# The first quad's second head pair: loaded as fp32 by two other queues and cast on VectorE

## The chip, the cores and the metric

The kernel runs on one core of one Trainium2 chip. The metric is the device time of one execution in microseconds (us). Five engines run their own instruction streams: TensorE (PE in the profile; PEld is its weight load), VectorE (DVE), ScalarE (ACT), GpSimd (POOL) and SyncE (SP). DMAs are issued from the queues of POOL, SP and ScalarE. Only those issued by POOL convert a type on the way here; the ones that SP and ScalarE issue at the start move fp32 as it is.

## The reference

Attention with an extra one in the softmax's sum, over 8 batches, 12 heads, 448 positions, head size 64, followed by a feed-forward layer with squared ReLU:

```python
scores = scale * np.matmul(q, k.transpose(0, 1, 3, 2))
m = np.max(scores, axis=-1, keepdims=True)
e = np.exp(scores - m)
attn = e / (np.sum(e, axis=-1, keepdims=True) + np.exp(-m) + 1e-09)
x = (attn @ v).transpose(0, 2, 1, 3).reshape(B * S, H * D)   # 3584 x 768
h = x @ w_in                                                 # 768 x 2048
g = np.maximum(h, 0.0) ** 2
out = g @ w_out                                              # 3584 x 768, fp32
```

The inputs are fp32; the kernel multiplies in fp16.

## The kernel before, in words

The 12 heads of a batch are three quads of four heads; a quad has two head pairs, j = 0 and 1, and in a pair the two heads lie in partitions 0 to 63 and 64 to 127. For scores, q and k are needed with the head size in the partitions, so TensorE transposes them by matmuls against an identity (`ident`), and VectorE or ScalarE copies the result from PSUM to the tile `qk`.

The order of all work is written out by hand. Each step in the text `ORDER` (line 858) is a letter and its numbers, and each engine takes its own instructions of these steps in that order; a wait stands in the engine's way of everything behind it. The steps of the start that matter here (name 0 is q, 1 is k):

- `load_first_quad` (L121): SP loads q and ScalarE loads k of the first quad's pair j = 0, in two pieces each (columns 0 to 255, 256 to 447), as fp32, into the tile `raw`, which is an exponential tile (`et`) used early.
- `load_first_second` (L128): POOL loads q and k of pair j = 1 of the first quad, cast to fp16 on the way, to `flatq` and `flatk`. Then POOL makes the identity.
- `d0`, `d8`, `d1` and so on: further POOL loads. `d0` loads q and k of quad 1 of batch 0 (tile `nn`), `d8` v of quad 0, `d1` quad 2.
- `c` (`first_cast`, L220): casts a piece of `raw` to fp16, on ScalarE (last number 1) or VectorE (0).
- `t n,j,c` (`first_transpose`, L229): TensorE transposes a piece of pair j, with one idle matmul ahead; `u n,j,c,act` (`first_copy`, L238): the copy out of PSUM. The transposes use two PSUM buffers in turn.
- `s n` and `e n`: the scores of one piece (`half_scores`) and their exponential on ScalarE (`half_exp`, L255). Steps 0 to 3 and 12 to 15 are the first quad's (s0 and s1 need only pair 0, s2 and s3 pair 1; 12 on belong to the second half of the queries). The scores have two PSUM buffers.
- `T0,1,n` and `U`: transposes of quad 1's q and k out of `nn` (L208) and their copies (L218). They come behind s12 and ahead of s3 in TensorE's order.
- `b`, `y`, `z`, `n`, `x`, `p`: the sums, reciprocals and products with v of each half quad.

Behind this start the matmuls of attention, of `w_in` and of `w_out` of several batches are woven together; later batches are loaded through fp16 copies in DRAM and transposed by DMA.

Of the kernel before, what the change touches and what calls it, by code (L numbers as in the profile page):

```python
# [10 lines left out]
FP32 = mybir.dt.float32  # L11
FP16 = mybir.dt.float16
# [5 lines left out]
def kernel(  # L18
# [9 lines left out]
    nc = tc.nc  # L28

    B, H, S, D = q.shape  # L30
# [4 lines left out]
    RUN = 4  # L35
    NQ = H // 4
    KC = S // 64
# [16 lines left out]
    flat = ctx.enter_context(tc.tile_pool(name="flat", bufs=2))  # L54
    qk_pool = ctx.enter_context(tc.tile_pool(name="qk", bufs=2))
    e_pool = ctx.enter_context(tc.tile_pool(name="e", bufs=4))
# [18 lines left out]
    by_pairs = {n: t.rearrange("b (hp i) (p t) d -> b (i p) hp (t d)", i=2, t=KC)  # L75
                for n, t in (("q", q), ("k", k), ("v", v))}
# [4 lines left out]
    vns, qks, xts, naturals, stages = {}, {}, {}, {}, {}  # L81
# [37 lines left out]
                naturals[name, b, g] = parts[:, x, n].rearrange("p j (c d) -> p j c d", d=D)  # L119

    def load_first_quad():  # L121
        raw = e_pool.tile([128, RUN * S], FP32, name="et")[:, 0:2 * S].rearrange("p (n x) -> p n x", n=2)
        for c0, c1 in ((0, 4 * D), (4 * D, S)):
            nc.sync.dma_start(out=raw[:, 0, c0:c1], in_=by_pairs["q"][0, :, 0, c0:c1])
            nc.scalar.dma_start(out=raw[:, 1, c0:c1], in_=by_pairs["k"][0, :, 0, c0:c1])
        return raw.rearrange("p n (c d) -> p n c d", d=D)

    def load_first_second():  # L128
        for name in "qk":
            f = naturals[name, 0, 0, 1] = flat.tile([128, KC, D], FP16, name=f"flat{name}")  # L130
            nc.gpsimd.dma_start(out=f.rearrange("p c d -> p (c d)"), in_=by_pairs[name][0, :, NQ])

    def load_win(i, n):
        w = DF // n
# [82 lines left out]
        else:  # L217
            nc.vector.tensor_copy(dst, src)  # L218

    def first_cast(raw, name, c0, c1, act):  # L220
        if (name, 0, 0, 0) not in naturals:
            naturals[name, 0, 0, 0] = flat.tile([128, KC, D], FP16, name=f"flat{name}")
        f, src = naturals[name, 0, 0, 0][:, c0:c1], raw[:, "qk".index(name), c0:c1]
        if act:
            nc.scalar.activation(out=f, in_=src, func=AF.Copy)
        else:
            nc.vector.tensor_copy(f, src)

    def first_transpose(which, j, c0, c1):  # L229
        rows_ = slice(64 * j, 64 * j + 64)  # L230
        tp = tps[which, j, c0] = mp_tile(FP16)
        x, n = 64 - 64 * j, 128 * (c1 - c0)
        mm(aside()[x:x + 64, 0, 0:n], idle[:, x:x + 64], idle[:, 0:n], start=True, stop=True)
        for c in range(c0, c1):
            nc.tensor.transpose(tp[rows_, 128 * (c - c0):128 * (c - c0) + 128],
                                naturals[which, 0, 0, j][:, c, :], ident)
# [355 lines left out]
    one_b = consts.tile([128, 1], FP32)  # L592
    nc.vector.memset(one_b, 1.0 / GS)
    raw = load_first_quad()
    nc.scalar.preload_act_table_set("natural_log_exp_and_others")
    ident = consts.tile([128, 128], FP16)
    nc.vector.memset(ident, 0.0)
    load_first_second()
    make_identity(nc, ident, nomemset=True)
    NW = 4  # L600

# [4 lines left out]
    def fill(n):  # L606
        wp = mp_tile()
        for _ in range(n):
            mm(wp[:, 0:S], idle[:, 0:128], idle[:, 0:S], start=True, stop=True)
# [203 lines left out]
    def halves(b):  # L813
# [3 lines left out]
    STEPS = {  # L817
        "W": lambda n: keep_warm(n),
        "f": lambda n: fill(n),
        "c": lambda n, c, act: first_cast(raw, "qk"[n], c, KC if c else 4, act),  # L820
        "t": lambda n, j, c: first_transpose("qk"[n], j, c, KC if c else 4),
        "u": lambda n, j, c, act: first_copy("qk"[n], j, c, KC if c else 4, act),
        "T": lambda b, g, n: transpose_one(b, g, "qk"[n]),
# [30 lines left out]
    def other_ring():  # L854
# [1 line left out]
        ring.append(ctx.enter_context(tc.tile_pool(name="ring", bufs=4, space=bass.MemoryType.PSUM)))  # L856

    ORDER = """
        d0 W8 d8 d1 c1,4,0 c0,0,1 t0,0,0 c1,0,1 t1,0,0 u0,0,0,0 t1,0,4 u1,0,0,0 c0,4,1 u1,0,4,1 t0,0,4 d2 s0 t0,1,0 u0,0,4,1 u0,1,0,0 t1,1,0
        u1,1,0,0 d10 d9 s1 t0,1,4 e0 t1,1,4 e1 s2 e2 u0,1,4,0 s12 e12 u1,1,4,0 T0,1,0 T0,1,1 U0,1,0,0,4,0 U0,1,1,0,4,0 U0,1,1,4,7,0  # L860
        U0,1,0,4,7,0 s3 s4 p2 p0 e3 b0,0 e4 s6 p1 d18 p3 s5 e6 e5 b0,1 b0,2 T0,2,0 b0,3 y0 T0,2,1 U0,2,0,0,4,0 z0 n0 U0,2,1,0,4,0 b1,0 s8
        U0,2,0,4,7,0 U0,2,1,4,7,0 x0 d3 d17 d16 b1,1 s9 d15 T1,0,1 e8 e9 U1,0,1,0,7,0 T1,0,0 U1,0,0,0,7,0 b2,0 s11 e11 s10 s13 e10 e13 s14 p8
# [232 lines left out]
```

## Time and profile before

| | us |
|---|---|
| median of 3 runs | 372.48 |
| lowest, highest | 372.31, 372.57 |
| profiled execution | 372.36 |
| its span (first to last instruction) | 370.3 |
| TensorE busy in the span | 361.7 |
| ScalarE, VectorE, POOL busy | 282.4, 275.7, 62.3 |

The granted clock of TensorE was 1.00 throughout. A row of the timeline reads: start, length, engine, line, operation, tiles, shape, count, and in brackets the idle time of that engine just ahead of it with what ended it. Rows of the chain read: start, length, what. The rows of stretches give each engine's busy time, then the clock, the share of the 16 DMA engines (over 1 where packets overlap) and GB/s. The rows of DMA issues end with the size of one and the median time from issue to landing.

### The profile page before, as it was taken

How to read it: one execution, taken by the hardware profiler on the slowest of the kernel's cores; microseconds unless marked ns; L12 is line 12 of the kernel's file. 1: busy time of each engine (PE TensorE's matmuls, PEld its weight loads, DVE VectorE, ACT ScalarE, POOL GpSimd, SP SyncE). 2: the span in 40 equal slices, each digit the busy share in tenths (PEclk: the TensorE clock that was granted, in tenths of full speed). 3: DMA queues.
4: the chain of work that ended last, by engine and by line, in shares of the span. 5: the costliest groups of instructions: out<-in, count | busy, mean ns of one | idle time of the engine just before them, and what ended most of it. 6: DMA issues, size and time to landing. Idle time of an engine off the chain costs nothing.

```text
span 370.3 us, 13666 instructions
## 1 busy us (share of the span) xinstructions
PE 361.7 (98%) x6024; PEld 248.8 (67%) x6024; DVE 275.7 (74%) x484; ACT 282.4 (76%) x413; POOL 62.3 (17%) x96
## 2 busy tenths in 40 slices
PE   8789999999999999999999999999999999999996
PEld 4566556669977755567799965557777765555664
DVE  3888898999987875867887874777878777885441
ACT  6899988987899645689999665679999748794221
POOL 8543350400400330400201060400200000000000
PEclk9999999999999999999999999999999999999999
DMA  8999999999777999905229669854212110001232
GB/s 138 203 205 205 204 198 206 226 225 189 154 146 133 190 181 191 134 2 114 62 58 156 154 118 180 162 64 99 61 53 66 47 62 5 2 0 44 86 85 88
DMA packets 75052, 45.31 MB, mean 122 GB/s; under 512 B 47473, under 2 KB 72945, under 8 KB 74993
## 3 DMA queue, kind: packets, MB, share of 16 engines
q0 software_dynamic: 24752, 22.62, 38.7%
q1 hardware_dynamic: 49952, 21.59, 27.0%
q8 instruction: 47, 0.77, 0.9%
q10 hardware_dynamic: 288, 0.23, 0.2%
q14 instruction: 13, 0.10, 0.1%
HBM read 45.69 MB, written 17.93 MB: 172 GB/s over the span
## 4 chain that ended last, share of the span: by engine, by line
PE 90%; ACT 4%; DVE 2%; DMA 2%; issue 1%; POOL 1%; POOLq 0%; DVEq 0%
PE mp L94 42%; PE mp L663 38%; PE sp L94 9%; ACT et L255 3%; DMA nn<-in_k_dram 2%; PE mp L208 1%; ACT rcp L373 1%; DVE qk L218 0%; ACT rcp L366 0%; DVE half L342 0%; DVE half L441 0%; DVE half L443 0%; DVE half L445 0%; DVE half L348 0%; DVE xt L485 0%
## 5 line engine op out<-in xcount | busy, mean ns | idle before, releaser
L255 ACT ACTIVATE et<-sp 128x896 f16<-128x896 f32 (+2 forms) x173 | 145.2, 899 | 7.6 <-PE sp L94 6.9
L94 PE MATMUL mp<-wout,gs 64*64 64x384 f16 (+1 forms) x2736 | 138.8, 322 | 0.2 <-issue 0.2
L94 PEld LDWEIGHTS <-gs 64*64 64x64 f16 (+1 forms) x2736 | 87.4, 107 | 21.7 <-issue 0.8
L663 PEld LDWEIGHTS <-win 128*128 128x128 f16 x480 | 46.4, 98 | 33.6 <-issue 1.2
L94 PE MATMUL sp<-qk 64*64 64x224 f16 (+1 forms) x1056 | 56.2, 273 | 2.3 <-issue 0.7
L663 PE MATMUL mp<-xt,win 128*128 128x448 f16 (+1 forms) x288 | 54.2, 329 | 0.0
L94 PEld LDWEIGHTS <-qk 64*64 64x64 f16 x1056 | 34.4, 114 | 14.5 <-issue 6.2
L189 POOL COPY flatq<-qk 64x384 f16<-64x384 f16 x20 | 15.3, 763 | 159.4 <-DMA qk<-stage_k 142.7
L94 PE MATMUL mp<-et,vn 64*64 64x448 f16 (+1 forms) x616 | 38.8, 345 | 0.0
L663 PE MATMUL mp<-et,win 128*128 128x448 f16 x144 | 32.8, 352 | 0.0
L576 DVE TENSOR_SCALAR ot<-mp 128x384 f32<-128x384 f32 x34 | 18.9, 556 | 18.0 <-PE mp L94 17.9
L663 PE MATMUL mp<-et,nn 128*128 128x448 f16 (+1 forms) x160 | 32.3, 350 | 0.0
L663 PEld LDWEIGHTS <-nn 128*128 128x128 f16 x216 | 21.0, 98 | 14.7
L666 ACT ACTIVATE qk<-mp 128x448 f32<-128x448 f32 (+1 forms) x33 | 16.8, 532 | 16.0 <-PE mp L663 15.9
L580 DVE SCALAR_TENSOR_TENSOR ot<-mp,ot 128x384 f32<-128x384 f32 x42 | 23.4, 556 | 6.7 <-ACT ot L574 4.0
L485 DVE TENSOR_TENSOR xt<-mp,rcp 128x448 f16<-128x448 f32 x42 | 24.2, 618 | 4.3 <-ACT rcp L464 2.2
L94 PEld LDWEIGHTS <-vn 64*64 64x64 f16 x756 | 22.7, 107 | 6.1 <-issue 0.5
L715 ACT ACTIVATE gs<-mp 128x448 f16<-128x448 f32 x28 | 14.2, 543 | 15.0 <-PE mp L663 13.3
L439 DVE TENSOR_TENSOR half<-et 128x1792 f16<-128x1792 f16 x21 | 23.0, 1097 | 1.2 <-ACT et L255 1.2
L660 DVE CUSTOM_DVE_ANT_0 gs<-mp,rcp 128x448 f16<-128x448 f32 x24 | 14.2, 619 | 13.0 <-ACT rcp L666 7.4
L441 DVE TENSOR_TENSOR half<-half,et 128x1792 f16<-128x1792 f16 x21 | 22.8, 1085 | 0.7 <-DVE half L439 0.5
L710 ACT ACTIVATE gs<-gs 128x448 f16<-128x448 f16 (+1 forms) x36 | 22.4, 657 | 1.1 <-DVE gs L660 1.1
(102 smaller groups left out, 450.2 us busy)
## 6 DMA issues: line engine op xcount, KB each, us to landing
out_dram<-ot SPq DMA_DIRECT2D x52, 96.0 KB, 3.5
out_dram<-ot SPq DMA_DIRECT2D x19, 192.0 KB, 2.0
win<-in_moe_w_in_dram POOLq DMA_DIRECT2D x8, 384.0 KB, 12.9
wout<-in_moe_w_out_dram POOLq DMA_DIRECT2D x4, 768.0 KB, 11.8
vn<-in_v_dram POOLq DMA_DIRECT2D x10, 288.0 KB, 5.6
stage_q<-in_q_dram POOLq DMA_DIRECT2D x4, 676.0 KB, 11.6
stage_k<-in_k_dram POOLq DMA_DIRECT2D x4, 676.0 KB, 14.4
nn<-in_q_dram POOLq DMA_DIRECT2D x8, 224.0 KB, 7.9
```

Of the source, the lines that this page charges most:

```text
L94: return nc.tensor.matmul(out_, lhsT, rhs, start=start, stop=stop)
L189: nc.gpsimd.tensor_copy(km[rows_].rearrange("p h (x o) -> p h x o", o=2)[:, :, :, odd], src[:, :, S // 2 - 32:S // 2])
L255: nc.scalar.activation(out=out_, in_=in_, func=AF.Exp, scale=scale)
L439: nc.vector.tensor_add(esq[m], a[:, 0:w], a[:, w:2 * w])
L441: nc.vector.tensor_add(esq[m], esq[m], z[:, 0:w])
L485: nc.vector.tensor_mul(xts[b][:, 2 * g + i, :], xqs[m][i][:, 0:S], zqs[m][:, i, :])
L576: nc.vector.tensor_scalar(out=ot, in0=op[:, 0:w], scalar1=OUT_SCALE, scalar2=None, op0=ALU.mult)
L580: nc.vector.scalar_tensor_tensor(out=ot, in0=lo[:, 0:w], scalar=OUT_SCALE, in1=ot, op0=ALU.mult, op1=ALU.add)
L660: nc.vector._custom_dve(TENSOR_ADD_SAT, out=out_, in0=ps, in1=t, s0=3.0e38, s1=0.0)
L663: nc.tensor.matmul(out_, lhsT=lhsT, rhs=rhs, start=begins and first, stop=last, skip_group_check=not begins)
L666: nc.scalar.activation(out=t[:, 0:w], in_=src[:, 0:w], func=AF.Copy, scale=scale_)
L710: nc.scalar.activation(out=out_, in_=out_, func=AF.Square)
```

## The change

q and k of pair j = 1 of the first quad are no longer loaded by POOL. `raw` becomes twice as large, and SP and ScalarE each issue a third load, of 128 x 448 fp32, behind their first two. A new step `q n,act` casts one of the two to fp16 into `flatq` or `flatk`; both casts are on VectorE. q0,0 stands behind c0,4,1 and q1,0 behind d2, so on VectorE both come after the copies u0,0,0,0 and u1,0,0,0 and ahead of u0,1,0,0. POOL's first work is now the identity, and its first DMA is d0's. TensorE's order is unchanged; its first transposes of pair 1 wait for VectorE in place of a DMA.

```diff
     def load_first_quad():
-        raw = e_pool.tile([128, RUN * S], FP32, name="et")[:, 0:2 * S].rearrange("p (n x) -> p n x", n=2)
+        raw = e_pool.tile([128, RUN * S], FP32, name="et").rearrange("p (j n x) -> p j n x", j=2, n=2)
         for c0, c1 in ((0, 4 * D), (4 * D, S)):
-            nc.sync.dma_start(out=raw[:, 0, c0:c1], in_=by_pairs["q"][0, :, 0, c0:c1])
-            nc.scalar.dma_start(out=raw[:, 1, c0:c1], in_=by_pairs["k"][0, :, 0, c0:c1])
-        return raw.rearrange("p n (c d) -> p n c d", d=D)
-
-    def load_first_second():
-        for name in "qk":
-            f = naturals[name, 0, 0, 1] = flat.tile([128, KC, D], FP16, name=f"flat{name}")
-            nc.gpsimd.dma_start(out=f.rearrange("p c d -> p (c d)"), in_=by_pairs[name][0, :, NQ])
+            nc.sync.dma_start(out=raw[:, 0, 0, c0:c1], in_=by_pairs["q"][0, :, 0, c0:c1])
+            nc.scalar.dma_start(out=raw[:, 0, 1, c0:c1], in_=by_pairs["k"][0, :, 0, c0:c1])
+        nc.sync.dma_start(out=raw[:, 1, 0], in_=by_pairs["q"][0, :, NQ])
+        nc.scalar.dma_start(out=raw[:, 1, 1], in_=by_pairs["k"][0, :, NQ])
+        return raw.rearrange("p j n (c d) -> p j n c d", d=D)
...
-    def first_cast(raw, name, c0, c1, act):
-        if (name, 0, 0, 0) not in naturals:
-            naturals[name, 0, 0, 0] = flat.tile([128, KC, D], FP16, name=f"flat{name}")
-        f, src = naturals[name, 0, 0, 0][:, c0:c1], raw[:, "qk".index(name), c0:c1]
+    def first_cast(raw, name, j, c0, c1, act):
+        if (name, 0, 0, j) not in naturals:
+            naturals[name, 0, 0, j] = flat.tile([128, KC, D], FP16, name=f"flat{name}")
+        f, src = naturals[name, 0, 0, j][:, c0:c1], raw[:, j, "qk".index(name), c0:c1]
...
     nc.vector.memset(ident, 0.0)
-    load_first_second()
     make_identity(nc, ident, nomemset=True)
...
-        "c": lambda n, c, act: first_cast(raw, "qk"[n], c, KC if c else 4, act),
+        "c": lambda n, c, act: first_cast(raw, "qk"[n], 0, c, KC if c else 4, act),
+        "q": lambda n, act: first_cast(raw, "qk"[n], 1, 0, KC, act),
...
-        d0 W8 d8 d1 c1,4,0 c0,0,1 t0,0,0 c1,0,1 t1,0,0 u0,0,0,0 t1,0,4 u1,0,0,0 c0,4,1 u1,0,4,1 t0,0,4 d2 s0 t0,1,0 u0,0,4,1 u0,1,0,0 t1,1,0
+        d0 W8 d8 d1 c1,4,0 c0,0,1 t0,0,0 c1,0,1 t1,0,0 u0,0,0,0 t1,0,4 u1,0,0,0 c0,4,1 q0,0 u1,0,4,1 t0,0,4 d2 q1,0 s0 t0,1,0 u0,0,4,1 u0,1,0,0 t1,1,0
```

## The prediction

> **What bounds the kernel now.** I read the page's busy times and the summary of the chain that ended last, then that chain in order of time, then the timeline of each engine over the first 16 us, where the change sits. From the page:
>
> ```profile
> span 370.3 us, 13666 instructions
> PE 361.7 (98%) x6024; PEld 248.8 (67%) x6024; DVE 275.7 (74%) x484; ACT 282.4 (76%) x413; POOL 62.3 (17%) x96
> PE 90%; ACT 4%; DVE 2%; DMA 2%; issue 1%; POOL 1%; POOLq 0%; DVEq 0%
> ```
>
> TensorE is busy 98% of the span and holds 90% of the chain. A change at the start can therefore do one thing only: move the time at which TensorE's unbroken work begins. The chain in order of time (start, length, what):
>
> ```profile
> 1.25 0.47 POOL flatq L131
> 1.93 0.56 POOL flatk L131
> ...
> 3.59 6.19 DMA nn<-in_k_dram
> 9.83 0.60 PE mp L208 x14
> 10.45 0.95 DVE qk L218 x3
> ...
> 15.41 5.19 ACT et L255 x7
> ...
> 33.37 2.39 PE mp L94 x12
> ```
>
> The reader is to see four legs. POOL issues q and k of the first quad's second head pair (flatq, flatk), then q and k of quad 1 (nn). The load of nn's k takes 6.19 us from its issue, and TensorE's transposes of it start at 9.83. VectorE copies them out, ScalarE's exponentials carry the chain from 15.41, and TensorE has it from 33.37 to the end. So the two POOL issues that the change removes stand on the chain, ahead of the load that ends its second leg. Whether their going is worth anything depends on what the chain's next-latest neighbours are at 9.83. ScalarE:
>
> ```profile
> 1.65 1.28 ACT L595 ACT_TABLE_LOAD   x1 [1.65 <-PEq L1079]
> 3.68 0.42 ACT L225 ACTIVATE flatq<-et 128x256 f16<-128x256 f32 x1 [0.75 <-DMA et<-in_q_dram]
> 6.27 1.77 ACT L255 ACTIVATE et<-sp 128x896 f16<-128x896 f32 x3
> 8.33 1.73 ACT L255 ACTIVATE et<-sp 128x896 f16<-128x896 f32 x2 [0.29 <-PE sp L94]
> 10.86 3.22 ACT L255 ACTIVATE et<-sp 128x448 f16<-128x448 f32 x5 [0.81 <-PE sp L94]
> 15.41 5.18 ACT L255 ACTIVATE et<-sp 128x896 f16<-128x896 f32 x7 [0.18 <-PE sp L94]
> ```
>
> ScalarE works almost without a break from 6.27 on. The two exponentials of 8.33 end at 10.06; then it idles 0.81 us until 10.86 for the scores of step s3. After 10.86 there is only 0.18 us of idle time at 15.41. So the most this stage can give is 0.81 + 0.18 = 0.99 us, less what the steps before 8.33 lose. TensorE in the same stretch:
>
> ```profile
> 6.16 0.41 PE L235 MATMUL mp<-ident,flatq 128*64 128x128 f16 x4
> 6.41 0.39 PE L235 MATMUL mp<-ident,flatk 128*64 128x128 f16 x4
> 6.74 0.47 PE L94 MATMUL sp<-qk 64*64 64x224 f16 x6
> 7.14 0.35 PE L235 MATMUL mp<-ident,flatq 128*64 128x128 f16 x3
> 7.72 0.76 PE L94 MATMUL sp<-qk 64*64 64x224 f16 x16
> 8.69 0.58 PE L208 MATMUL mp<-ident,nn 128*64 128x128 f16 x14 [0.21 <-DMA nn<-in_q_dram]
> 9.83 0.58 PE L208 MATMUL mp<-ident,nn 128*64 128x128 f16 x14 [0.55 <-DMA nn<-in_k_dram]
> 10.35 0.97 PE L94 MATMUL sp<-qk 64*64 64x224 f16 x14
> ```
>
> In order: step t0,1,0 (transposes of flatq's second half pair, 6.16), t1,1,0 (flatk's, 6.41), s1 (6.73), t0,1,4 (7.14), s2 and s12 (7.72), T0,1,0 (nn's q, 8.69, which waited for its load), T0,1,1 (nn's k, 9.83, likewise), s3 (10.35). s3 reads nothing of nn: it only stands behind T0,1,1 in TensorE's order. That is why a load sets ScalarE's 0.81 us.
>
> **The change part by part.** *POOL.* Removed: two DMA issues, 0.70 + 0.56 us.
>
> ```profile
> 1.25 0.70 POOL L131 DMA_DIRECT2D flatq<-in_q_dram  x1 [0.80 <-POOLq L1079]
> 1.93 0.56 POOL L131 DMA_DIRECT2D flatk<-in_k_dram  x1
> 2.61 0.29 POOL masks.py:199 TENSOR_SCALAR_AFFINE_SELECT ident<-ident 128x128 f16<-128x128 f16 x1
> 2.86 0.74 POOL L118 DMA_DIRECT2D nn<-in_q_dram  x1
> 3.59 0.73 POOL L118 DMA_DIRECT2D nn<-in_k_dram  x1
> ```
>
> All POOL work behind them moves up by 1.26 us: the identity (2.61, needed by TensorE's first transposes, which come after the cast of 3.68) to 1.35, nn's q from 2.86 to 1.60, nn's k from 3.59 to 2.33, and the issues after them alike. POOL's later waits are for landings eight of its own DMAs back, and these move with the issues.
>
> *The loads.* The DMA engines' share by stretch (the last two columns):
>
> ```profile
> 2.00:3.00 1.00, 1.00 (x4) 0.44 (x3) 0.00 (x0) 0.93 (x1) 0.88 (x3) 1.00 0.87 259
> 3.00:4.00 1.00, 1.00 (x5) 0.26 (x3) 0.08 (x1) 0.32 (x1) 1.00 (x2) 1.00 1.20 281
> 4.00:5.00 1.00, 0.87 (x11) 0.57 (x12) 0.81 (x3) 0.66 (x3) 1.00 (x2) 1.00 1.10 107
> ```
>
> The plain fp32 loads ran at 259 to 281 GB/s mixed with others; the engines were already at a share of 1.10 to 1.20 from 3 us. The removed and the added loads read the same 2 x 229 KB, so the engines' work until nn's k is complete stays about as it was, and only the 1.26 us of issue is gained, at most: nn's k at 9.78 - 1.26 = 8.5 us; at least nothing (9.8), if the engines are the limit throughout. I take about 9.0, between the two, as the share of 1.10 is nearer to full. nn's q was late at 8.69 and comes by 7.4 to 8.7.
>
> The new loads are the third issue on SP's and ScalarE's queues. A pair of issues takes 0.90 us there, so the third goes out at about 0.74 + 0.90 = 1.6 and ends near 2.1. On ScalarE it pushes the table load from 1.65 to 2.1, ending at 3.4: hidden behind the wait until 3.68 (0.75 us of idle time, of which 0.45 is used; without that cover it would cost 0.45).
>
> ```profile
> 0.74 0.90 SPq L124 DMA_DIRECT2D et<-in_q_dram  x2
> et<-in_q_dram SPq DMA_DIRECT2D x1, 128.0 KB, 2.9
> flatk<-in_k_dram POOLq DMA_DIRECT2D x1, 112.0 KB, 4.0
> ```
>
> The first two loads of each queue are done by 4.0 (the cast at 3.92). The new ones follow in the same queues: 459 KB at 281 GB/s is 1.6 us, so from about 3.7 to 5.3 with nn's q sharing the engines. Bounds: 1.6 + 2.9 = 4.5 by the fp32 rows' time to landing; 1.6 + 5.8 = 7.4 if they take as long as nn's q did (2.86 to 8.69). I take 5.4; the removed flatk, on the more crowded queue, would give 1.6 + 4.0 = 5.6, near it.
>
> *VectorE.* Two casts 128x448 fp32 to fp16, q0,0 and q1,0, go in behind u1,0,0,0 and ahead of u0,1,0,0:
>
> ```profile
> 3.92 0.49 DVE L227 CAST flatk<-et 128x192 f16<-128x192 f32 x1 [2.90 <-DMA et<-in_k_dram]
> 4.60 0.75 DVE L245 COPY qk<-mp 64x512 f16<-64x512 f16 x2 [0.19 <-PE mp L235]
> 6.63 0.77 DVE L245 COPY qk<-mp 64x512 f16<-64x512 f16 x2 [1.29 <-PE mp L235]
> ...
> L485 DVE TENSOR_TENSOR xt<-mp,rcp 128x448 f16<-128x448 f32 x42 | 24.2, 618 | 4.3 <-ACT rcp L464 2.2 <-PE mp L94 1.8
> L580 DVE SCALAR_TENSOR_TENSOR ot<-mp,ot 128x384 f32<-128x384 f32 x42 | 23.4, 556 | 6.7 <-ACT ot L574 4.0
> ```
>
> VectorE is free from 4.60 + 0.75 = 5.35 until 6.63, so 1.28 us of cover. One cast: the only row alike is 0.49 for 192 columns. Bounds: 0.38, half of the 0.75 that two copies of 512 fp16 columns took at 4.60, and 0.49 x 448 / 192 = 1.14, were all of that row in proportion to its columns. Between, the rows for 448 and 384 columns give a slope of (618 - 556) / 64 = 0.97 ns a column, so 0.49 + 256 x 0.97 ns = 0.74. I take that: it is built on the nearest row. So q0,0 runs 5.40 to 6.14 and q1,0 to 6.88. The exponential tile that the larger fp32 tile shares a pool with is next written at 15.41, long after; SP has nothing queued behind its third issue but output stores.
>
> *What stands behind the casts.* t0,1,0 starts at 6.2, as before (it follows s0). t1,1,0 waits for q1,0: from 6.41 to 6.95, and s1 behind it from 6.73 to about 7.3. u0,1,0,0 moves from 6.63 to 6.88, and the copy u1,1,0,0 from an end at 7.40 to 7.8. t1,1,4 needs its buffer, so s2 starts at about 8.25 (before 7.72): 0.53 us late. The exponentials of s0 and s1 ended at 6.27 + 1.77 = 8.04, which is 1.30 after s1's start; now at 8.6. That end frees the scores buffer for s12, which before was through at 7.72 + 0.76 = 8.48, 0.44 later; now at 9.05. T0,1,0 follows (its load is there at 8.7 at the latest), and 0.55 later, at 9.6, T0,1,1, if its load is there. Before it was 9.83. s3 keeps its 0.52 behind it: 10.12 in place of 10.35. Its scores reached ScalarE 0.51 after that: 10.64. ScalarE's exponentials of s2 and s12 begin 0.53 late, at 8.86, and end at 10.59. So it takes s3 at 10.64 in place of 10.86.
>
> *Sum.* Before, TensorE could have begun T0,1,1 at 8.48 + 0.55 = 9.03: its two waits cost 9.83 - 9.03 = 0.80 us, which earlier landings give back. The late second half pair takes 0.57 of that. Left at ScalarE: 10.86 - 10.64 = 0.22 us, and as ScalarE has next to no idle time after it, all of it reaches 33.37 and the end. Against the profiled execution (372.36 us, of which 2.06 lie outside its span of 370.3): 372.1. The median, 372.48, is 0.12 above that execution, so 372.2 to 372.3; I say 372.2.
>
> [...] The cast of 192 columns ran from 3.92 to 4.41, and POOL's issue of 3.59 ended at 4.32: the cast ended 0.09 us after it. [...]
>
> **The rivals.**
> [...]
> 2. *The load of nn's k is not earlier*, the change then not doing what it says, since the engines were busy anyway. T0,1,1 stays at 9.83, TensorE is ready at 9.6: 372.5, no change. For: shares of 1.10 to 1.20 from 3 us. Against: the k load's 6.19 us, of which its own packets are a fraction.
> 3. *The new loads come late* (the slower side). Place: the wait of q0,0 and q1,0. Every step from t1,1,0 to s3 is behind them on VectorE and TensorE. Price: each 0.1 us of landing past 5.4 costs 0.1, after the 0.22 of gain is eaten; from 6.4 on the kernel is slower by more than 0.74 us. With the time that nn's q took, landing at 7.4: 2.0 - 0.22 = 1.8 us, 374.3; at 6.6, 373.5. For: in the same crowded stretch nn's q took 5.8 us and nn's k 6.2. Against: the fp32 rows, 2.7 to 2.9.
> 4. *The casts are hidden* (faster). Casts of 0.38 and landing by 5.4 end q1,0 at 6.2, ahead of 6.41, and nothing behind moves. T0,1,0 then starts at 8.5, T0,1,1 at 9.03, s3 at 9.55, and ScalarE takes it at 10.06, when its own work ends: 0.80, and the 0.18 at 15.41 may go too: 371.7 to 371.5. For: cover of 1.28 us. Against: it needs both the low bound of the cast and nn's k by 9.0.
>
> **How the numbers follow.** 0.74 us, 0.2%, is about what a measurement of this kernel can tell from no change. Chances: the sum 0.30, rival 1 0.10, rival 2 0.08 (all within 0.2%: 0.48); rival 3 0.28; rival 4 0.24, all of it counted as over 0.2%, though its first 0.80 is close to the line. The likeliest, the sum, is 372.2, its own range 371.9 to 372.6. The range from 371.5 (rival 4 whole) to 373.6 (a landing at about 6.8) leaves out the worst third of rival 3, 1 in 10, and something for what I have not seen, another 1 in 10.
>
> **What would show it.** Right: POOL's first nn issue near 1.6; two casts of 0.6 to 0.8 us starting at 5.4; t1,1,0 near 6.95; T0,1,1 near 9.6 without a DMA wait; the exponential of s3 near 10.6 and an unchanged length from there to the end. Wrong: a cast that starts after 6, with "DMA et" as its releaser (rival 3); T0,1,1 still waiting for nn's k (rival 2); t1,1,0 unmoved (rival 4); or TensorE's first break after 33 us being a DMA, a place where I see none now.

## The result, and the profile after

| | us |
|---|---|
| before, median of 6 executions beside the changed kernel | 372.52 (372.31 to 373.17) |
| changed kernel, median of 6 | 374.98 (373.84 to 376.12) |
| ratio, 95% interval | 1.0058 (1.0041 to 1.0076) |
| profiled execution of the changed kernel, its span | 374.29, 372.5 |

The kernel became slower by 2.5 us. 372.2 was forecast, with a range up to 373.6. The page of the changed kernel, its summary of busy times and of the chain that ended last:

```profile
span 372.5 us, 13671 instructions
PE 362.5 (97%) x6024; PEld 249.8 (67%) x6024; DVE 277.3 (74%) x486; ACT 282.3 (76%) x413; POOL 63.3 (17%) x94
PE 86%; ACT 8%; DVE 2%; DMA 2%; issue 1%; SPq 0%; DVEq 0%
```

TensorE's busy time grew by 0.8 us (361.7 before), the span by 2.2: the rest is idle time of TensorE. (0.6 of the 0.8 need not be the change's: the full clock was first granted at 4.76 us in this execution and at 3.48 in that of before. Ahead of it the idle matmuls of 512 columns follow each other every 0.43 us and take 0.63, behind it one takes 0.38 to 0.41, and the nine at the start take 4.13 us in place of 3.54. The clock of 1.00 that was given for before is thus that from 3.48 us on.) The chain in order of time (start, length, what):

```profile
1.68 5.59 DMA et<-in_q_dram
...
16.04 5.19 ACT et L252 x7
...
34.01 2.39 PE mp L94 x12
```

Before, POOL's issues and the load of nn's k led the chain. Now the new fp32 load of q leads it, 5.59 us long, and then VectorE's cast. ScalarE's exponentials start at 16.04 (15.41 before) and TensorE takes the chain at 34.01 (33.37 before): 0.64 us late. The timeline of the start:

```profile
1.41 0.86 POOL L118 DMA_DIRECT2D nn<-in_q_dram  x1
2.15 1.28 ACT L592 ACT_TABLE_LOAD   x1 [2.15 <-issue]
2.26 0.74 POOL L118 DMA_DIRECT2D nn<-in_k_dram  x1
...
7.30 0.40 DVE L224 CAST flatq<-et 128x448 f16<-128x448 f32 x1 [1.57 <-DMA et<-in_q_dram]
7.61 0.39 DVE L224 CAST flatk<-et 128x448 f16<-128x448 f32 x1
7.75 0.24 PE L232 MATMUL mp<-ident,flatq 128*64 128x128 f16 x1 [0.80 <-DVE flatq L224]
8.66 0.72 POOL L106 DMA_DIRECT2D vn<-in_v_dram  x1 [1.35 <-DMA nn<-in_q_dram]
8.91 0.79 ACT L252 ACTIVATE et<-sp 128x448 f16<-128x448 f32 x2 [1.34 <-PE sp L94]
10.07 0.97 PE L205 MATMUL mp<-ident,nn 128*64 128x128 f16 x28
```

In order: POOL's issues moved up by 1.45 and 1.33 us (1.41 and 2.26). The table load follows the new third issue, at 2.15, and is hidden. VectorE's first cast did not start at 5.40 but at 7.30, after 1.57 us of idle time that the load of q ended. TensorE's transposes of flatq, at 6.16 before, began at 7.75. ScalarE's next exponentials waited 1.34 us. The transposes of nn (10.07, all 28 in one piece) waited for no load any more. From the issues to the landings, of the loads of SP and ScalarE (size of one, time to landing):

```profile
et<-in_k_dram ACTq DMA_DIRECT2D x1, 224.0 KB, 5.4
et<-in_q_dram SPq DMA_DIRECT2D x1, 224.0 KB, 5.6
et<-in_q_dram SPq DMA_DIRECT2D x1, 96.0 KB, 3.0
```

The first two loads of each queue take 2.9 to 3.1 us (2.7 to 2.9 before). The third takes 5.4 to 5.6, nearly twice as long.

The rest of this execution's loss comes later. Compared matmul by matmul, TensorE is 0.64 us behind the execution of before at 34 us, 1.15 at 82, 1.72 at 112 and 1.88 from 182 to the end. The timeline of TensorE, of the changed kernel and of the one before, shows short breaks that no releaser ends:

```profile
80.20 0.36 PE L94 MATMUL mp<-wout,gs 64*64 64x384 f16 x4 [0.34 <-issue]
110.79 0.36 PE L94 MATMUL mp<-wout,gs 64*64 64x384 f16 x4 [0.74 <-issue]
```

```profile
109.08 0.36 PE L94 MATMUL mp<-wout,gs 64*64 64x384 f16 x4 [0.18 <-issue]
```

These cost 1.08 us in this execution and 0.18 in the one before. They come at the same two matmuls in every trace of either kernel, if they come: 0.34 and none in the second trace of the changed kernel, under 0.1 and 0.49 to 0.60 in two traces of kernels without the wait or with POOL held. They differ from execution to execution of one kernel; what makes them, and whether the change makes them longer on average, is open.

### The profile page after: what moved, and what is told of

It reads as the page before. It is cut to its first block, busy times and chain, and to the rows that moved or that the text cites. A ratio compares the mean times of both kernels' runs of the same rounds, so it can differ in the third digit from the quotient of the medians.

```text
span 372.5 us, 13671 instructions
## 1 busy us (share of the span) xinstructions
PE 362.5 (97%) x6024; PEld 249.8 (67%) x6024; DVE 277.3 (74%) x486; ACT 282.3 (76%) x413; POOL 63.3 (17%) x94
## 4 chain that ended last, share of the span: by engine, by line
PE 86%; ACT 8%; DVE 2%; DMA 2%; issue 1%; SPq 0%; DVEq 0%
PE mp L94 39%; PE mp L659 37%; PE sp L94 8%; ACT et L252 7%; DMA et<-in_q_dram 2%; PE mp L205 1%; ACT rcp L370 1%; DVE qk L215 0%; ACT rcp L363 0%; DVE half L339 0%; PE xp L94 0%; ACT rcp L458 0%; PE mp L232 0%; SPq L124 0%; ACT rcp L461 0%
## 5 line engine op out<-in xcount | busy, mean ns | idle before, releaser
L186 POOL COPY flatq<-qk 64x384 f16<-64x384 f16 x20 | 17.2, 861 | 159.0 <-DMA qk<-stage_k 122.1
```

Source lines behind the costliest of these rows:

```text
L186: nc.gpsimd.tensor_copy(km[rows_].rearrange("p h (x o) -> p h x o", o=2)[:, :, :, odd], src[:, :, S // 2 - 32:S // 2])
```

## The experiments

Two theories to begin with. **A: late loads.** The new loads land late because POOL's queue starts beside them, and the wait of VectorE for them costs everything. **B: something else** (the casts, the clock of TensorE, POOL's work being earlier) costs the time, and the lateness is mostly hidden. All comparisons that follow are with executions of the kernel before on the same chip, 16 to 29 of them, medians 372.76 to 373.01.

### The changed kernel again

> The changed kernel once more, for a second trace of it. In its first trace TensorE's matmuls stand 1.58 us behind those of before at the first transpose of pair 1, 0.66 behind from the transposes of nn's k on, 1.14 behind from 79 us, 1.72 from 109 us and 1.88 from 180 us. Theory L (the late loads are the cause of all): all these steps come again, within 0.2 us. Rival F (the steps at 79, 109 and 180 us are breaks of another origin that only chance or the new phase brings): the 1.58 and 0.66 come again, the later steps move or change size by over 0.3 us. Timed: 374 to 376, in two groups about 1.7 us apart with granted clocks of 1.000 and 0.995, if the clock is a part of its own.

Measured: 374.82 us (373.21 to 375.51, 6 executions), ratio 1.0050 (1.0030 to 1.0069). Its timeline at the cast:

```profile
8.50 0.40 DVE L224 CAST flatq<-et 128x448 f16<-128x448 f32 x1 [2.89 <-DMA et<-in_q_dram]
8.95 0.24 PE L232 MATMUL mp<-ident,flatq 128*64 128x128 f16 x1 [2.11 <-DVE flatq L224]
```

The cast waited 2.89 us, the loads took 6.7 to 6.8 us, and TensorE stood still for 2.11 us. The later steps did not come again as they were, which speaks for rival F: TensorE was 1.87 us behind the first trace of before from the transposes of nn's k on, and 2.22 at the end. A third trace of the changed kernel, with twelve executions, stands beside the late VectorE below.

> The changed kernel again, beside the other three on the same chip: 374.4 to 375.2, landings of the new loads between 7 and 8.5 us. Beside the late VectorE it tells what of the loss is not the lateness of the start: a difference of over 0.7 us says that something else is in it, one under 0.4 that the start is all.

Measured: 374.08 us (373.29 to 376.29, 12 executions), ratio 1.0036 (1.0016 to 1.0055), a little under the 374.4 that was expected at least; its cast began at 8.05 us. So in three traces the new loads let the cast start at 7.30, 8.05 and 8.50.

### POOL held back

```diff
+    spare = consts.tile([128, 128], FP16)
+    nc.vector.memset(spare, 0.0)
+    for _ in range(5):
+        make_identity(nc, spare, nomemset=True)
```

These lines stand ahead of the identity; the second run has 9 in place of 5.

> POOL makes five more selects like the identity's (0.29 us each) on a spare tile ahead of its first load, so that nn's loads go out about 1.3 us later, near 2.7, as in the kernel before; the fp32 loads of pair 1 stay as they are. Theory L1 (the fp32 loads land late because nn's loads share the DMA engines): they land by 5.8 in place of 7.25, pair 1's first transpose starts by 6.4 in place of 7.75, and the time falls to about 372.5 to 373.2. Rival L2 (the fp32 loads are slow by themselves): they land at 6.8 or later, and the time stays at 374 or above.

> As e2, with nine more selects in place of five: POOL's first load is issued near 4.4 (e2 3.0, the changed kernel 1.4). Theory L1 (the fp32 loads are late because POOL's loads run beside them): all of their packets fall before POOL's begin, and they land at 4.9 to 5.4 (e2 6.2 to 6.4, the changed kernel 7.2 to 8.5); pair 1's first transpose starts behind s0, at 6.1 to 6.5; nn's k lands at 11 or later and costs 1 us or more instead. Rival L2: the fp32 loads land at 6 or later here too.

Measured with five: 373.94 us (7 executions), ratio 1.0032 (1.0018 to 1.0045), in place of the 372.5 to 373.2 expected. With nine: 374.15 us in a single execution, which tells little. The timelines:

```profile
3.87 0.74 POOL L118 DMA_DIRECT2D nn<-in_k_dram  x1
6.20 0.39 DVE L224 CAST flatq<-et 128x448 f16<-128x448 f32 x1 [0.37 <-DMA et<-in_q_dram]
10.49 0.58 PE L205 MATMUL mp<-ident,nn 128*64 128x128 f16 x14 [0.85 <-DMA nn<-in_k_dram]
```

```profile
5.45 0.74 POOL L118 DMA_DIRECT2D nn<-in_k_dram  x1
6.20 0.40 DVE L224 CAST flatq<-et 128x448 f16<-128x448 f32 x1 [0.47 <-DMA et<-in_q_dram]
9.21 1.05 PE L205 MATMUL mp<-ident,nn 128*64 128x128 f16 x28
```

The cast starts at 6.20 in both, 1.1 to 2.3 us earlier than in the changed kernel. So POOL's loads beside the new ones cost these 1.1 to 2.3 us (less in some executions: in the first trace of the next section the new loads, with POOL beside them, took 5.0 and 5.5 us, against 4.5 and 4.7 here and 5.4 to 6.8 in the changed kernel). The packet records of the nine traces with both new loads bear this out: on the whole, the later POOL's first packet starts, the earlier the last packet of the new loads ends.

| us | | | | | | | | | |
|---|---|---|---|---|---|---|---|---|---|
| POOL's first packet starts | 3.61 | 3.67 | 3.83 | 3.90 | 3.94 | 4.18 | 4.36 | 4.59 | 6.17 |
| the new loads' last packet ends | 7.93 | 8.08 | 7.70 | 7.70 | 7.90 | 6.85 | 6.90 | 5.84 | 5.85 |

The last two columns are POOL held by five and by nine. What is left is not POOL's: held back by another 1.6 us, POOL changed nothing, and 6.20 is still 0.8 later than the 5.40 of the sum. The time fell by less than the landing because another wait took over: with five selects TensorE waits 0.85 us for nn's k (10.49).

The moved bytes (GB/s in forty slices of the first 24 us, 0.6 us each), for the changed kernel, for POOL held by five and by nine:

```profile
GB/s 0 0 5 116 353 307 182 139 246 257 199 193 197 203 200 203 205 200 206 202 203 203 222 193 197 204 205 200 212 203 205 212 202 202 218 196 200 202 210 205
```

```profile
GB/s 0 0 7 79 342 363 297 290 155 194 194 182 134 79 114 158 167 199 202 202 205 220 196 196 206 200 206 201 205 207 205 189 210 222 196 190 196 201 206 203
```

```profile
GB/s 0 0 7 97 356 342 224 233 215 57 42 106 205 197 200 167 197 206 196 205 199 196 176 197 199 199 199 205 204 199 187 172 198 215 166 172 191 196 205 198
```

With POOL beside it the rate falls from 353 in the slice from 2.4 us to 139 in that from 4.2; with POOL held by five it stays at 290 to 363 until 4.8 and falls when POOL's own loads have begun. With nine, no packet of POOL runs beside the new loads, and the rate is still no more than 215 to 233 from 3.6 to 5.4, where the sum had 281. So about half of the 0.8 us is a rate that was taken too high: 459 KB at 224 GB/s, the mean of these three slices, take 2.0 us in place of 1.6. The other half is the 0.35 us from the last packet (5.85) to the cast (6.20), for which the sum had nothing.

The row of nn's k is the other finding: issued at 5.45, it landed after 4.2 us, at 9.65; issued at 3.87 it was waited for until 10.49. When nn's k lands does not follow from when POOL issues it alone.

### The wait taken away

```diff
-        f, src = naturals[name, 0, 0, j][:, c0:c1], raw[:, j, "qk".index(name), c0:c1]
+        f, src = naturals[name, 0, 0, j][:, c0:c1], raw[:, 0, "qk".index(name), c0:c1]
```

> The casts of pair 1 read the fp32 of pair 0, which is there early, so that nothing waits for the new loads; these are still made, and not read. Left out: the use of the right q and k for heads 6 and 7 of batch 0. Theory L (the wait is the cost, not the loads' traffic): first transpose of pair 1 at about 6.2 to 6.6, the exponential of s3 near 10.1 to 10.4, a matmul stream 0.3 to 0.8 us ahead of the kernel before at 33 us; time 371.7 to 372.4. Rival (the earlier loads of POOL or the traffic cost something elsewhere): the stream at 33 us is not ahead of before, time 372.8 or more.

> e3 once more (pair 1 cast from pair 0's fp32; the new loads made and not read), for a second trace: its first trace was 0.79 us ahead of before at the start, but its median of twelve no better than before. Theory V (what the start gains, chance in the loads and TensorE's later breaks take or give): the start is again 0.6 to 0.8 ahead of the first trace of before, and the rest differs. Rival (the start itself is often not ahead): nn's k lands after 9.0 and the start is ahead by less than 0.4.

Measured: 372.99 us (371.87 to 373.66, 12 executions), ratio 1.0002 (0.9991 to 1.0014); the second run, one execution, 373.39. The timeline of the first, and that of the second at the transposes of nn's k:

```profile
5.48 0.61 DVE L224 CAST flatq<-et 128x448 f16<-128x448 f32 x1
6.01 0.37 DVE L224 CAST flatk<-et 128x448 f16<-128x448 f32 x1
8.54 4.03 ACT L252 ACTIVATE et<-sp 128x896 f16<-128x896 f32 x6 [0.29 <-PE sp L94]
8.62 1.00 PE L205 MATMUL mp<-ident,nn 128*64 128x128 f16 x28
```

```profile
10.08 0.58 PE L205 MATMUL mp<-ident,nn 128*64 128x128 f16 x14 [0.61 <-DMA nn<-in_k_dram]
11.11 3.22 ACT L252 ACTIVATE et<-sp 128x448 f16<-128x448 f32 x5 [0.73 <-PE sp L94]
```

All of the change is in these kernels but the wait, and the loss is gone. That is theory A: the wait for the new loads is the whole of it. But the gain that the sum counted on did not come either, and the time is not the 371.7 to 372.4 that was expected with it. TensorE is 0.79 us ahead of the first trace of before at 33 us in the first trace and 0.25 behind in the second: in the first nn's k was there (8.62, no DMA wait) and ScalarE ran through, in the second TensorE waited 0.61 us for it and ScalarE 0.73, though POOL had issued it 1.3 us earlier than before. Over twelve executions the earlier issue is worth nothing that can be measured.

### The kernel before again, and the identity alone

> The kernel before once more, for a second trace of it. If its first trace is typical, nn's k lands near 9.8, the exponential of s3 starts near 10.9, TensorE takes the chain over within 0.3 us of 33.4, and its break without a named releaser at 109 us is 0.1 to 0.3 us long. If the start varies from execution to execution by itself, as the times of 371.9 to 373.3 suggest, these move by 0.4 us or more.

Measured: 372.90 us, one execution. Its transposes of nn's k and the exponential behind them:

```profile
10.41 0.58 PE L208 MATMUL mp<-ident,nn 128*64 128x128 f16 x14 [0.54 <-DMA nn<-in_k_dram]
11.45 3.22 ACT L255 ACTIVATE et<-sp 128x448 f16<-128x448 f32 x5 [0.69 <-PE sp L94]
```

These stood at 9.83 and 10.86 in the trace on which the prediction was built. POOL had issued the load at the same time (3.58 and 3.59), and it took 6.8 us in place of 6.2. So the start of one and the same kernel varies by 0.6 us from one execution to the next, and the sum had been made against an early one.

```diff
-    make_identity(nc, ident, nomemset=True)
...
+        "m": lambda n: make_identity(nc, ident, nomemset=True),
...
-        d0 W8 d8 d1
+        d0 m0 W8 d8 d1
```

> The kernel before with one thing moved: POOL makes the identity behind nn's q and k, not ahead of them, so these are issued 0.37 us earlier (0.29 for the select and its gap) and the identity is ready at about 4.2. If nn's k is what sets the start of before, ScalarE takes s3's exponential 0.2 to 0.35 us earlier and the time is 0.1 to 0.35 below before. If the DMA engines, not POOL's issues, set its landing: no change. If the first transposes, which need the identity from 4.15 on, wait for it: 0.1 to 0.2 slower.

Measured: 372.51 us (371.69 to 374.64, 12 executions), ratio 0.9996 (0.9979 to 1.0012): the place of the identity is worth nothing that can be told.

### One of the two loads alone

```diff
-        nc.scalar.dma_start(out=raw[:, 1, 1], in_=by_pairs["k"][0, :, NQ])
...
+    f = naturals["k", 0, 0, 1] = flat.tile([128, KC, D], FP16, name="flatk")
+    nc.gpsimd.dma_start(out=f.rearrange("p c d -> p (c d)"), in_=by_pairs["k"][0, :, NQ])
     make_identity(nc, ident, nomemset=True)
```

> One part of the change alone: q of pair 1 goes by SyncE's queue and VectorE's cast, k of pair 1 stays with POOL, ahead of the identity. One fp32 load fewer beside POOL's, and POOL's loads of nn move up by 0.7 in place of 1.26 us. If the queues crowding each other make the new loads late, q's should land nearer 6 than 7.5 us and the time be about half way, 373.2 to 373.9. If any fp32 load behind two others is late, whatever runs beside, it lands past 7 and the time is 374.2 or more. If the loss hangs on the start of POOL's work being earlier, 373.2 or less.

Measured: 373.71 us (372.43 to 373.97, 12 executions), ratio 1.0012 (0.9995 to 1.0029).

```profile
6.92 0.63 DVE L223 CAST flatq<-et 128x448 f16<-128x448 f32 x1 [1.09 <-DMA et<-in_q_dram]
```

The median is 0.8 us over that of before on the same chip, where the whole change (the third run of it) had 1.2; the interval just reaches no change. With one load fewer the cast starts at 6.92. This bears out that the loads make each other late, and does not prove it.

### VectorE late, without the loads

Theory A says that lateness is all. So the kernel before was given the lateness alone, with its own loads:

```diff
+    def late(n, times):
+        for _ in range(times):
+            nc.vector.tensor_copy(spare, raw[:, 0])
+        f = naturals["qk"[n], 0, 0, 1]
+        nc.vector.tensor_copy(f, f)
...
-        c0,4,1 u1,0,4,1 t0,0,4 d2 s0 t0,1,0
+        c0,4,1 q0,6 u1,0,4,1 t0,0,4 d2 q1,0 s0 t0,1,0
```

> The kernel before, its loads untouched; VectorE alone is made late: six casts into a spare tile and a copy of flatq in place (then one of flatk) at the places where the changed kernel has its two casts. They take some 0.31 us each, so that the copies of flatq and flatk end near 7.7 and 8.0 us, as the casts of the changed kernel did, and TensorE's first transposes of pair 1 come near 7.6. Nothing of the result is left out. If the lateness of VectorE at the start is what the new loads cost, all of the 2.0 to 2.5 us should come back: 374.5 or more. If the start carries only what its own waits show (0.7 to 1.2 us), 373.4 to 374.0, and the rest belongs to something else that the new loads bring, or to chance. If the start hides the lateness, 372.6 to 373.0.

The second run of this kind has four casts in place of six.

> The kernel before with VectorE made late by four casts in place of six: the copies of flatq and flatk end near 8.4 and 8.7 us, the first transposes of pair 1 near 8.4, about as in the three traces of the changed kernel (7.75, 8.95, 8.49). TensorE waits about 1.5 us. If lateness alone, of whatever origin, is what the change costs, the time is that of the changed kernel, 374.0 to 375.0, and the granted clock is under 0.998 in some executions and 1.00 in others, about 1 in 4. If the loads cost something beside it, 373.6 or less.

Measured with six casts: 377.25 us (376.51 to 377.83, 5 executions), ratio 1.0110 (1.0090 to 1.0129). With four: 375.26 us (373.85 to 376.05, 7 executions), ratio 1.0057 (1.0036 to 1.0077). The six casts took 3.50 us where 1.9 were expected, so that run was later than meant:

```profile
5.75 3.50 DVE L821 CAST spare<-et 128x448 f16<-128x448 f32 x6
9.49 0.31 PE L235 MATMUL mp<-ident,flatq 128*64 128x128 f16 x1 [2.44 <-DVE flatq L823]
```

The run with four has the lateness of the changed kernel, and its time:

```profile
5.76 2.37 DVE L821 CAST spare<-et 128x448 f16<-128x448 f32 x4
8.36 0.24 PE L235 MATMUL mp<-ident,flatq 128*64 128x128 f16 x1 [1.30 <-DVE flatq L823]
12.10 1.71 PE L208 MATMUL mp<-ident,nn 128*64 128x128 f16 x28
```

Its first transposes of pair 1 come at 8.36 (8.49 in the third trace of the changed kernel). 1.0057 against 1.0058 and 1.0036 to 1.0050 for the changed kernel: lateness alone, with the old loads, costs about as much as the change. The agreement is in part chance, for five of its seven executions have a lowered clock (below), and the median is over the 374.0 to 375.0 expected; the two with the full clock took 373.85 and 374.16, 0.85 and 1.16 us over the full-clock median of before on the same chip (373.00). But the last row shows something that A had not said: the 28 transposes of nn take 1.71 us, where they take 0.97 in the changed kernel's trace. A stretch of this execution (the columns after the busy times are the granted clock, the DMA share and GB/s):

```profile
9.00:12.50 3.50, 3.50 (x46) 2.45 (x46) 1.34 (x4) 1.46 (x3) 2.06 (x3) 0.50 1.23 196
```

The trace's records of the clock have it fall to half at 8.71 us and come back at 15.53: 6.83 us at half. In the run with six casts it is the same, from 9.09 to 15.92.

### TensorE kept busy

Now the question was whether the clock fell because TensorE stood idle. The run with six casts, with ten matmuls on an idle tile while TensorE waits; and the changed kernel with four, twice:

```diff
-        t0,0,4 d2 q1,0 s0 t0,1,0
+        t0,0,4 d2 q1,0 s0 W10 t0,1,0
```

> The kernel before with VectorE made late as in the run before (six casts into a spare tile, flatq and flatk copied in place), and with ten matmuls on an idle tile ahead of t0,1,0, so that TensorE is busy in most of the 2.44 us in which it waited. The lateness is the same. If the clock was halved because TensorE stood idle, the granted clock is 1.00 in every execution, the scores and transposes from 9.5 to 15.9 us run at their full rate, and the time falls from 377.25 by the 3.4 us that 6.83 us at half the clock had cost, or by a little more or less: 373.6 to 375.0. If the idle time is not the reason, 377 stays, with granted clocks of 0.991.

> Four idle matmuls of 512 columns (0.21 us each) ahead of the first transpose of pair 1 fill 0.85 us of the 1.10 that TensorE is idle there while it waits. Theory C (in about half the executions the idle time costs the granted clock a further stretch of some 3.5 us at half speed): no execution with a clock under 0.998 is left, the times lie within 0.6 us of each other, median about 374.2. Rival (the clock falls for another reason): executions at 0.995 and 375.5 or more still come, median 375.

> The changed kernel with four matmuls on an idle tile ahead of t0,1,0, again and in more executions. If idle time at TensorE is what makes some executions of the changed kernel fall to a granted clock of 0.995, none does here (it was 6 of 24 without these matmuls), no execution is over 375.0, and the median is 373.9 to 374.3. If these executions are chance, some two or three of twelve are at 0.995 and over 375.3.

Measured: the late kernel 375.58 us (375.03 to 375.90, 6 executions), ratio 1.0063 (1.0044 to 1.0081), in place of 377.25. The changed kernel 374.15 us (373.68 to 374.75, 6 executions) and 374.17 us (372.96 to 374.86, 10 executions), ratios 1.0038 (1.0023 to 1.0053) and 1.0031 (1.0016 to 1.0045). The late kernel (a stretch, and a row of its timeline), then the changed one (second run):

```profile
9.00:12.50 3.50, 2.76 (x60) 2.07 (x61) 2.33 (x7) 1.35 (x3) 1.69 (x3) 1.00 1.25 196
12.04 0.97 PE L208 MATMUL mp<-ident,nn 128*64 128x128 f16 x28
```

```profile
6.65 1.38 PE L94 MATMUL xp<-const-bfloat16-1.0 128*128 128x512 bf16 x5
8.04 0.39 DVE L224 CAST flatq<-et 128x448 f16<-128x448 f32 x1 [2.20 <-DMA et<-in_q_dram]
8.48 0.24 PE L232 MATMUL mp<-ident,flatq 128*64 128x128 f16 x1 [0.45 <-DVE flatq L224]
```

With the same lateness the clock stays at 0.999 to 1.00, in all six executions, and the late kernel is 1.67 us faster. (The late kernel's trace holds no record of the clock; that it ran at the full rate is seen by the 28 transposes of nn, 0.97 us.) It missed the 373.6 to 375.0 that I had expected: the six casts were even later in its trace (transposes at 9.79 in place of 9.49), and half a clock need not cost half of its length: with the full clock TensorE is idle for 1.17 of the 7.0 us from 9.00 to 16.00. The granted clock of every execution, by kernel:

| kernel | executions | of these with a mean clock of 0.990 to 0.995 |
|---|---|---|
| before (the four later comparisons) | 80 | 7 |
| changed | 24 | 6 |
| changed, TensorE kept busy | 16 | 0 |
| before, VectorE late by four casts | 7 | 5 |
| before, late by six casts | 5 | 5 |
| the same, TensorE kept busy | 6 | 0 |

With TensorE kept busy neither kernel has a low clock (0 of 16 and 0 of 6 executions). For the late one chance would give 5 of 5 against 0 of 6 once in 462 draws. For the changed one it is weaker: 6 of 24 against 0 of 16 comes by chance once in 28, and against the 7 of 80 of before once in 22. That the run with four casts has 5 of 7 where I had expected 1 in 4 is not explained; its seven executions are few.

So the changed kernel's loss has two parts. The 18 executions of it with the full clock have a median of 374.14, the 73 of before 372.82: lateness costs 1.3 us (1.2 to 1.8 in the three comparisons taken one by one). The other 6 have a median of 376.01: where the clock falls as well, 1.9 more. None of the three traces of the changed kernel is of this kind, so that its clock falls at this wait is concluded from the kernels kept busy. Half of the six executions of the first comparison were of this kind, hence its 2.5 us.

### s3 ahead of the transposes of nn's k

```diff
-        u1,1,4,0 T0,1,0 T0,1,1 U0,1,0,0,4,0 U0,1,1,0,4,0 U0,1,1,4,7,0
-        U0,1,0,4,7,0 s3 s4
+        u1,1,4,0 T0,1,0 s3 T0,1,1 U0,1,0,0,4,0 U0,1,1,0,4,0 U0,1,1,4,7,0
+        U0,1,0,4,7,0 s4
```

> The kernel before with one step moved: s3, which reads nothing of quad 1, stands ahead of T0,1,1 on TensorE, so the wait for nn's k no longer stands ahead of ScalarE's exponential of s3. If that wait is what the change could have won at most, ScalarE's idle time ahead of its exponentials at 10.9 falls from 0.8 to 0.1 or less, and the time is 371.7 to 372.1. If the step that waits next (s4, behind the copies of T0,1,1) gives the same wait back, 372.4 to 372.8.

Measured: 373.11 us (372.28 to 373.84, 12 executions), ratio 0.9999 (0.9984 to 1.0013): no change, and over both ranges expected.

```profile
8.82 2.41 ACT L255 ACTIVATE et<-sp 128x896 f16<-128x896 f32 x4 [0.29 <-PE sp L94]
...
11.74 2.54 ACT L255 ACTIVATE et<-sp 128x896 f16<-128x896 f32 x3 [0.50 <-PE sp L94]
```

ScalarE's four exponentials now run in one piece from 8.82, s3's among them, so the 0.81 us of before are gone from there. They turn up in the next step: the one of s4 waits 0.50 us at 11.74, for s4 stands behind the copies of T0,1,1. No version here beats the kernel before by more than the noise.

## Why the prediction was wrong

*What bounds the kernel, and that the start is carried to the end:* right. 0.63 us at 16.04 is 0.64 at 34.01.

*POOL moves up by 1.26 us, and the third issue pushes only hidden work:* right, by a little more (1.45 and 1.33), and the table load went to 2.15 with ScalarE's next cast waiting for its load as before.

*nn's k is there by about 9.0:* no. Issued at 2.26, it took 7.3, 7.8 and 7.5 us in the three traces of the changed kernel and landed at 9.6, 10.1 and 9.8; in the two of before it landed at 9.8 and 10.4. It was in time only because TensorE came later still (10.5 to 11.7); without the wait it was in time once (at 9.04) and waited for once (to 10.08). Rival 2 was nearer: 1.33 us of earlier issue moved the landing by some 0.3 us (the means are 9.8 and 10.1), and an issue 1.86 us later than before (5.45 against 3.59) did not make it later (9.65).

*The new loads land at 5.4:* the step that failed. It took the start (3.7) from the first loads' end and 1.6 us from the rate of the fp32 loads, 281 GB/s, as if the rate held while POOL's queue started. In the three traces the casts found them at 7.30 to 8.50, and t1,1,0 and T0,1,1, forecast at 6.95 and 9.6, came at 8.05 and 10.5 in the first. Of this, 1.1 to 2.3 us go when POOL is held back, and 0.8 us remain, shown by the cast at 6.20: even with no packet of POOL's beside them the new loads ran at 215 to 233 GB/s, not at 281. The range of bounds, 4.5 to 7.4, took its upper end from nn's q in the one trace there was and was too low by a microsecond. Rival 3 named the mechanism, place and sign, and I gave it 0.28. Its price was too high: it says 1.68 us for a landing of 7.3 (0.1 for each 0.1 past 5.4, less 0.22), and 0.66 was measured at T0,1,1. The casts make up for most: the second one ended 0.70 us after the landing (7.30 to 8.00) where the sum had 1.48, and with that the same formula gives 0.90. That 1.68 comes near the 1.93 us between the two profiled executions (374.29 and 372.36) is luck: only 0.64 of these is the start.

*Casts of 0.74 us:* mis-sized for where they ran. In the changed kernel they took 0.40 and 0.39 us, and met no issue of POOL's, which idled for 1.35 us ahead of its issue of 8.66. Beside issues such casts were drawn out in other runs (0.48 to 0.69 us), and so was the row on which the 0.74 was built: the cast of 192 columns took 0.49 there, 0.26 or 0.27 in seven other traces and 0.41 to 0.53 in six. Rows of the late kernel (six casts):

```profile
6.72 1.39 DVE L821 CAST spare<-et 128x448 f16<-128x448 f32 x2
7.16 0.72 POOL L118 DMA_DIRECT2D nn<-in_k_dram  x1
7.88 0.72 POOL L106 DMA_DIRECT2D vn<-in_v_dram  x1
```

Two casts take 1.39, 0.69 each in place of 0.39; one took 0.63 in the kernel with q alone and 0.61 without the wait. Each ends 0.21 to 0.23 us after the end of an issue that it met (here at 8.11, where the issue of 7.16 ends at 7.88); POOL's 0.72 did not grow. So in these rows the cost of the meeting is on the cast, up to 0.30 us of it. Not every cast that met an issue was held up: without the wait, a cast of 0.37 at 6.01 ran whole inside the issue of 5.82. In the three traces of the changed kernel this cost nothing, since the late landing put both casts into a pause of POOL's.

*From s2 to s3 by the rows, 0.22 us of gain:* fell with the landing. That all 0.80 us of TensorE's waits are to be had was right only for the trace on which it was built; with s3 moved ahead, 0.50 of it came back one step later.

*What I had not seen:* the clock. The price of a wait at TensorE was counted as its length alone. In the late kernels the clock halved for 6.83 us, with four casts at 8.71, behind the wait of 1.30 us, with six at 9.09, inside that of 2.44; by the mean clocks of 0.995 the changed kernel's six executions have half of that (an estimate: 3.41 x 0.5 / 374 = 0.005), and they are 1.9 us slower. Half a clock for 3.41 us can cost 1.71 us at most, so the rest must be something else, a longer wait perhaps. The prediction's last line of what could go wrong named a DMA wait after 33 us, and not this.

What stays open: why the rate of the new loads falls to 215 to 233 GB/s without POOL beside them, where that of the first loads reaches 342 to 356 in the same trace; what decides whether the clock falls behind a wait; and the breaks of 0.1 to 0.75 us at 80 and 110 us.

## What to carry to other kernels

A load's time to landing was not its bytes over the best rate seen: the new loads took 5.4 to 6.8 us where the sum had 3.8 (1.6 to 5.4). In a crowded start, price a new load with the slowest neighbour that shares its moment (nn's q: 5.8 us) and add what the next queue's start takes from it (here 1.1 to 2.3 us), above all where an engine's instruction waits for it and others are queued behind. Price a wait of TensorE twice: its own length, and the clock that may fall with it. Here the clock fell with waits of 1.30 and 2.44 us and not with those of 1.79 and 2.11; a few matmuls on an idle tile removed the second part (6 of 24 executions against 0 of 16). And before a sum of tenths of a microsecond is made, a second trace of the same kernel tells how far its start wanders, here 0.6 us.

## What the runs showed of the hardware

- The full clock was first granted between 3.5 and 6.5 us after the span's start, by execution: at 3.48 in the first trace of before and at 4.76 in that of the changed kernel, while in the second trace of before three transposes at 5.88 still took 0.48 us in place of 0.33. In the two traces that have a fall (the late kernels) it then stayed full for 3.41 us and was half for 6.83. In the run with four casts the full stretch ahead of the fall (5.29 to 8.71 us) holds an unbroken idle time of TensorE of 1.30 us (7.06 to 8.36), in the run with six casts 2.04 us (from 7.05 on). In both it is the first stretch at the full clock; whether that matters is open.
- The length of TensorE's idle time alone does not decide whether the clock falls: with 1.30 us it fell in the run with four casts, and the third trace of the changed kernel has 1.79 us unbroken (6.70 to 8.49) and the second 2.11 (6.84 to 8.95), and both kept their clock (1.00).
- VectorE's fp32 to fp16 cast of 128x448 took 0.39 us, or 0.31 from one to the next, and 0.48 to 0.69 where it was drawn out beside POOL's DMA issues, which themselves stayed at 0.72 to 0.78.
- New fp32 loads of 2 x 229 KB, third in the queues of SP and ScalarE, had their last packet at 5.85 us when POOL's first came at 6.17, and at 7.70 to 8.08 when it came at 3.61 to 3.94.
- A load issued by POOL 1.86 us later (nn's k, 5.45 in place of 3.59) landed at 9.65, and at 9.8 and 10.4 in two traces of the kernel before.
